# Transposing attention outputs to token rows: transpose instructions and a separate narrow logit product in place of one product with an identity-and-gate matrix

## The chip, the cores and the metric

The kernel runs on one core of one Trainium2 chip. The metric is the device time of one execution in microseconds, as the median of several runs. Below, PE is the matmul engine (its weight loads are listed apart as PEld), DVE, ACT and POOL are the vector, scalar and GpSimd engines, and SP issues most of the DMAs.

## What is computed

Linear attention over blocks feeds a top-1 mixture of experts. Shapes: q, k, v are (4, 8, 768, 64); x has N = 3072 tokens of 512 numbers; 8 experts, w1 (8, 512, 1024), w2 (8, 1024, 512).

```python
# attention, per batch and head, per block b of the sequence
intra = (qb @ kb.T * Dmask) @ vb
inter = (qb * lam_pow) @ kv_state
out[block] = intra + inter
kv_state = lam_block * kv_state + (kb * rev_pow).T @ vb
# x: the outputs of the 8 heads side by side, one row of 512 for each token
logits = x @ w_gate + modality_bias[modality_id]
e_idx = argmax(logits); gate_w = softmax(logits)[e_idx]
out[token] = gate_w * (relu(x @ w1[e]) @ w2[e])   # e = e_idx of the token
```

## The kernel before, in words

The kernel has two stages. **Attention** works on groups of 128 tokens (24 groups, numbered g), two groups to a pair (12 pairs, numbered j). Heads are taken in four pairs (`NP` = 4); the two heads of a pair lie in the two halves of the 128 partitions. Each pass of the loop `for j in range(1, pairs)` computes, on PE, the scores of two groups (`scores`, L239), what the carried state gives to the outputs (`from_state`, L285), what the masked scores give (`outputs`, L292, once for each group), and the products for the next state (`key_values`, L259). Between these stand four steps of the generator `turned(j - 1)`, which turn the outputs of the pair before from columns into token rows.

`outputs` leaves a group's result in SBUF as `xt`: 128 partitions (the two heads' 64 features), four head pairs, 128 tokens. Each step of `turned` calls `tokens`, which takes two of the four head pairs of one group: for each it makes two matmuls (L303), one for each half of 64 tokens, whose weights are that part of `xt` and whose moving operand is `iw`, 136 columns wide: a 128-wide identity (with its halves swapped for the second group of a pair, whose heads lie the other way round) and the 8 columns of the gate. So 4 head pairs x 136 = 544 numbers leave for each token: 512 features and four partial sums for the 8 logits. One copy for each step moves 2 x 136 columns from PSUM to SBUF (`xn`, L305), and after the second step of a group a DMA writes the rows, 544 numbers each, to the table `xs` in DRAM (L307). `gates` (L312) sums the four partial logits on DVE, and `route` picks the expert, two passes later.

PE's order is fixed by hand: `pinned` ties each instruction to the one before it on its engine. In a pass of the loop PE runs: scores, from_state, a step of `turned`, outputs of the first group, a step, outputs of the second group, a step, key_values, a step. PSUM tiles named "x" and "kv" have one buffer each; the steps use "x", and the second of them "kv" (as key_values does). "s" and "o" have two buffers. For the last pair the four steps stand after the loop, mixed with `turn_part` (L630), real transposes of the first gathered expert tile, and they use "s".

**Experts**: a tile of 256 tokens of one expert is gathered from `xs` by row (L595), turned by `turn_part`, and multiplied with `w1` and `w2`, each split in two parts (L643, L646, L647). Two tiles with few rows are done apart, with transposes (L689, L764) and on column tiles 64 and 32 wide (L678, L703).

Of the kernel before, what the change touches and what calls it, by code (L numbers as in the profile page):

```python
# [6 lines left out]
F32 = mybir.dt.float32  # L7
# [8 lines left out]
P = 128  # L16
B, H, S, D = 4, 8, 768, 64
NP = H // 2
NC = S // P
HB = 2  # L20
LOADS = 3
N = B * S
E, DM, F = 8, 512, 1024
# [10 lines left out]
LIST = THIN + MAX_WIDE + 2  # L34
PAD = 4096
SW = 8
ROW = DM + H // 2 * E
EMPTY = E * CAP // TT


def linear_attention_moe(tc, qkv, lam, modality, wg, mbias, w1, w2, out):
    nc = tc.nc
    with ExitStack() as ctx:
        const = ctx.enter_context(tc.tile_pool(name="const", bufs=1))
        dram = ctx.enter_context(tc.tile_pool(name="dram", bufs=1, space=bass.MemoryType.DRAM))
        ps = ctx.enter_context(tc.tile_pool(name="ps", bufs=1, space=bass.MemoryType.PSUM))
        work = ctx.enter_context(tc.tile_pool(name="work", bufs=2))
# [6 lines left out]
        def behind(later, first, wait=True):  # L54

            info = (mybir.DependencyInfo(mybir.DependencyClass.Sync, mybir.DependencyReason.DATA) if wait else
                    mybir.DependencyInfo(mybir.DependencyClass.NoSync, mybir.DependencyReason.SCHED_ONLY))
            tc.add_manual_dep(later.ins, first.ins.name, info, reason="order")


        halves2 = [slice(hl * D, (hl + 1) * D) for hl in range(2)]
        pins = {}

        def pinned(op):

            if op.ins.engine in pins:
                behind(op, pins[op.ins.engine], wait=False)
            pins[op.ins.engine] = op
            return op
# [48 lines left out]
        ident = const.tile([P, P], F32, name="ident")  # L118
        make_identity(nc, ident)

        wgt = const.tile([P, HB, NP, E], F32, name="wgt")
# [5 lines left out]
            return op  # L127


        iw = const.tile([P, HB, NP, P + E], F32, name="iw")  # L130
        onesb = const.tile([P, P], BF16, name="onesb")
        lowb = const.tile([P, P], BF16, name="lowb")
        desc = const.tile([P, E], F32, name="desc")
# [5 lines left out]
        modf = const.tile([P, 2, B * NC], F32, name="modf")  # L139
        xs = dram.tile([N, ROW], F32, name="xs")  # L140
        inv = dram.tile([E * CAP + TT, SW], I32, name="inv")
# [2 lines left out]
        pad = const.tile([P, some, SW], I32, name="pad")  # L144

        def identities():
            for blk in range(HB):
                nc.gpsimd.memset(iw[:, blk], 0.0)
                for hl, r in enumerate(halves2):
                    nc.gpsimd.tensor_copy(out=iw[r, blk, :, halves2[hl ^ blk]],  # L150
                                          in_=ident[r, r].unsqueeze(1).to_broadcast([D, NP, D]))

        def routing_constants():
            for to, src in ((mod, modality), (mb, mbias.partition_broadcast(P))):
# [53 lines left out]
        logits, ranked, fades = [], [], []  # L208
# [40 lines left out]
        def key_values(gs):  # L249

            kp = ps.tile([P, HB, NP, D], F32, name="kv", bufs=1)
            mm = None
            for g in gs:
                if g % NC == NC - 1 or g >= ng:
                    continue
                vt, kd = loaded(g)[2], kds[g // HB][:, g % HB]
                for p in range(NP):
                    for hl, r in enumerate(halves2):
                        mm = pinned(nc.tensor.matmul(kp[r, g % HB, p, :], kd[:, p, hl, :],  # L259
                                                     vt[:, (2 * p + hl) * D : (2 * p + hl + 1) * D], start=True, stop=True))  # L260
            return kp, mm
# [33 lines left out]
            pinned(nc.scalar.copy(out=xt, in_=op[blk]))  # L295
            return xt, mm

        def tokens(g, hf, xt, xn, xp):
            blk = g % HB
            for i in range(2):  # L300
                p = hf * 2 + i
                for r in halves2:
                    mm = pinned(nc.tensor.matmul(xp[r, i, : P + E], xt[:, p, r], iw[:, blk, p, :], start=True, stop=True))  # L303
            cp = nc.scalar.copy if g < ng - HB or (g == ng - 1 and hf == 0) else nc.vector.tensor_copy
            pinned(cp(out=xn[:, blk, 2 * hf : 2 * hf + 2, :], in_=xp[:, :, : P + E]))  # L305
            if hf == 1:
                nc.scalar.dma_start(out=xs[g * P : (g + 1) * P, :], in_=xn[:, blk].rearrange("t p d -> t (p d)"))  # L307
            return mm

        def gates(j, xn, lg):  # L310
            c = HB * j % NC
            logits.append(pinned(nc.vector.tensor_reduce(out=lg[:, c : c + HB, :], in_=xn[:, :, :, P:].rearrange("p b q e -> p b e q"),  # L312
                                                         axis=AX, op=ALU.add)))

        def route(b, lg):
# [273 lines left out]
        def groups(cols):  # L589

            return [(t, min(P, cols - t * P)) for t in range(-(-cols // P))]
# [11 lines left out]
        def fetch_regs(lst, i, always):  # L603
            er = value(lst, 0, i, E - 1)
            if always:
                return er, {}
            cr = value(lst, 2, i, 1)
            return er, {"cond": cr}
# [16 lines left out]
        def turn_part(i, cols, before=None, pin=False):  # L625
            tp = ps.tile([P, 2, TT], F32, name=("x", "kv")[i], bufs=1)
            for j in range(2):
                kc = 2 * i + j
                for t, m in groups(cols):
                    mm = nc.tensor.transpose(out=tp[:, j, t * P : t * P + m],  # L630
                                             in_=xg[t][:m, kc * (P + E) : kc * (P + E) + P], identity=ident[:m, :m])
                    if before is not None:
                        behind(mm, before, wait=False)
                    elif pin:
                        pinned(mm)
            return tp[:, :, :cols], xh[i][:, :, :cols], xl[i][:, :, :cols], pin
# [123 lines left out]
        def turn_few(x, rows):  # L760
            m = x.shape[-1]
            tp = ps.tile([P, KC, m], F32, name=("x", "kv")[m // XT], bufs=1)
            for kc in range(KC):
                pinned(nc.tensor.transpose(out=tp[:, kc, :], in_=rows[:, kc * (P + E) : kc * (P + E) + P],  # L764
                                           identity=ident[:m, :m]))
            return pinned(nc.vector.tensor_copy(out=x, in_=tp))

        def quarters(t):
            return [t[:, i] for i in range(4)]
# [5 lines left out]
        def parts(dt):  # L775

            return [work.tile([P, 4, KC, TT], dt, name=nm, bufs=1) for nm in ("w1h", "w1l")]

        w1h, w1l = (quarters(t) for t in parts(F32R))
        xg = [const.tile([m, ROW], F32, name=f"xg{t}") for t, m in groups(TT)]  # L780
        xq = [const.tile([m, ROW], F32, name=f"xq{i}") for i, m in enumerate((XT, FEW))]
        xh = [const.tile([P, 2, TT], F32R, name=f"xh{i}") for i in range(2)]
# [38 lines left out]

        ng = B * NC
        pairs, per = ng // HB, NC // HB
        kds, qds, xts, xns, lgs = {}, {}, {}, {}, {}
        early = SOON * per + 2
        routed, slots, placing = None, [], None

# [5 lines left out]


        def turned(j):
            xns[j] = work.tile([P, HB, NP, P + E], F32, name="xn", bufs=2)
            if j == pairs - 1:
                xp = [ps.tile([P, HB, 2, 256], F32, name="s", bufs=2) for _ in range(2)]
            for blk in range(HB):
                for hf in range(2):  # L840
                    if j < pairs - 1:
                        at = ps.tile([P, 2, 256], F32, name="kv" if hf and (j == pairs - 2 or j > 0 and blk == 0) else "x", bufs=1)
                    yield tokens(HB * j + blk, hf, xts[HB * j + blk], xns[j], xp[hf][:, blk] if j == pairs - 1 else at)

        def gated(j):
            b, c = divmod(j, per)
            if c == 0:
                lgs[b] = work.tile([P, NC, E], F32, name="lg", bufs=2)
            gates(j, xns.pop(j), lgs[b])
            return (b, *route(b, lgs.pop(b))) if c == per - 1 else None  # L850

        def more(j):
            if j < pairs:
                halves[j] = load_half(j)

        identities()
        clearing = clear_table(loads)
        c0, c1 = slice(0, 1), slice(1, 2)
# [17 lines left out]
        kp, _ = key_values([0])  # L876
# [1 line left out]
        xts[0], _ = outputs(0, pts[0], op)  # L878
        from_state(0, op, qds.pop(0))
        xts[1], _ = outputs(1, pts[1], op)  # L880
        pinned(nc.scalar.copy(out=iw[:, :, :, P:], in_=wgt))
        qds[1] = queries(1, c0, eng=nc.gpsimd)
        kp, _ = key_values([1])
        carried(1, kp)
        more(LOADS)
        for j in range(1, pairs):
# [20 lines left out]
            if j == 1:  # L907
                from_state(1, op, qds[1], range(1))
                next(turns)
                kp, _ = key_values(gs[:1])  # L910
                carried(gs[0], kp)
                keys(1, c1, kds[1])
            else:
                from_state(j, op, qds.pop(j))
                mm = next(turns)
# [7 lines left out]
            if j > 1:  # L923
                routed = gated(j - 2)
# [17 lines left out]
            kp, _ = key_values((gs[1], gs[1] + 1))  # L942
            mm = next(turns)
# [7 lines left out]
            if j == early:  # L951
                er, _ = fetch_regs(listA, 0, True)
# [4 lines left out]
            elif j == early + 2:  # L957
# [20 lines left out]
        hh, hl = ([t[:, i] for t in (work.tile([P, HB, 2, TT], F32R, name=f"{nm}{k}", tag=tag, bufs=2) for k in range(2))  # L978
                   for i in range(HB)] for nm, tag in (("hh", "pt"), ("hl", "kd")))
# [165 lines left out]
```

## Time and profile before

| | us |
|---|---|
| median of 3 runs | 412.56 (412.09 to 412.8) |
| the profiled execution | 410.96 |
| its span, first to last instruction | 408.6 |
| PE busy | 395.2 (97%) |
| DVE busy | 251.3 (61%) |
| ACT busy | 182.2 (45%) |
| POOL busy | 118.9 (29%) |

The profiled execution lasts 410.96 us, of which 2.4 us lie outside its span. Attention takes the span's first 105 us, the experts the rest; the last matmul ends near 397 us. Groups of instructions are named by line, engine and tiles; a matmul's form is given as rows x columns of the array that it uses (128*64 is all rows and half of the columns). A float32 matmul that is not a transpose is recorded as two instructions.

### The profile page before, as it was taken

How to read it: one execution, taken by the hardware profiler on the slowest of the kernel's cores; microseconds unless marked ns; L12 is line 12 of the kernel's file. 1: busy time of each engine (PE TensorE's matmuls, PEld its weight loads, DVE VectorE, ACT ScalarE, POOL GpSimd, SP SyncE). 2: the span in 40 equal slices, each digit the busy share in tenths (PEclk: the TensorE clock that was granted, in tenths of full speed). 3: DMA queues.
4: the chain of work that ended last, by engine and by line, in shares of the span. 5: the costliest groups of instructions: out<-in, count | busy, mean ns of one | idle time of the engine just before them, and what ended most of it. 6: DMA issues, size and time to landing. Idle time of an engine off the chain costs nothing.

```text
span 408.6 us, 9571 instructions
## 1 busy us (share of the span) xinstructions
PE 395.2 (97%) x3838; PEld 354.4 (87%) x3838; DVE 251.3 (61%) x430; ACT 182.2 (45%) x275; POOL 118.9 (29%) x125
## 2 busy tenths in 40 slices
PE   8999999999999999999999999999999999999990
PEld 3999899899998976989989898999989898998970
DVE  6777886978889714683746648273655738373610
ACT  2232243236654514582735547373644638273610
POOL 6701054452575610421230303122130402202000
PEclk9999999999999999999999999999999999999995
DMA  7999999994901291211073667111020211101000
GB/s 280 402 379 357 389 373 335 345 391 157 335 18 55 58 415 58 66 55 53 27 256 129 202 226 253 52 57 52 5 77 27 65 42 47 51 3 42 13 30 18
DMA packets 22374, 63.28 MB, mean 155 GB/s; under 512 B 6400, under 2 KB 6944, under 8 KB 20275
## 3 DMA queue, kind: packets, MB, share of 16 engines
q1 hardware_dynamic: 14000, 42.77, 28.9%
q0 software_dynamic: 4864, 13.15, 9.6%
q10 hardware_dynamic: 3458, 6.69, 4.3%
q8 instruction: 32, 0.52, 0.5%
q14 instruction: 20, 0.16, 0.1%
HBM read 90.87 MB, written 14.07 MB: 257 GB/s over the span
## 4 chain that ended last, share of the span: by engine, by line
PE 45%; issue 34%; POOL 7%; DMA 6%; DVE 4%; ACT 1%; POOLq 1%; SPq 1%; another core or an unknown queue 0%; DVEq 0%
PE s L239 5%; POOL out_dram L719 4%; PE o L292 4%; PE s L643 4%; PE s L646 4%; PE s L647 4%; PE x L303 3%; DMA idx<-inv 3%; PE o L285 3%; PE o L643 3%; PE o L646 3%; PE o L647 3%; POOL xg L595 2%; PE kv L259 2%; DMA xg<-xs,idx 2%
## 5 line engine op out<-in xcount | busy, mean ns | idle before, releaser
L643 PE MATMUL s<-xh,w1h 128*128 128x256 f32 x384 | 108.8, 283 | 0.0
L646 PE MATMUL s<-xl,w1h 128*128 128x256 f32 x384 | 108.5, 282 | 0.0
L647 PE MATMUL s<-xh,w1l 128*128 128x256 f32 x384 | 107.9, 281 | 0.0
L661 DVE SCALAR_TENSOR_TENSOR hl<-s,hh 128x512 fp32r<-128x512 f32 x48 | 33.2, 691 | 85.4 <-ACT hh L660 85.4
L643 PE MATMUL o<-w2h,hh 128*128 128x512 f32 x192 | 75.8, 395 | 0.0
L647 PE MATMUL o<-w2h,hl 128*128 128x512 f32 x192 | 74.8, 390 | 0.0
L646 PE MATMUL o<-w2l,hh 128*128 128x512 f32 x192 | 74.8, 389 | 0.0
L647 PEld LDWEIGHTS s<-xh,w1l 128*128 128x128 f32 x384 | 72.8, 190 | 0.0
L643 PEld LDWEIGHTS s<-xh,w1h 128*128 128x128 f32 x384 | 72.0, 187 | 0.9 <-ACT xn L305 0.3
L646 PEld LDWEIGHTS s<-xl,w1h 128*128 128x128 f32 x384 | 72.2, 188 | 0.4
L560 DVE TENSOR_TENSOR w2l<-raw,w2h 128x1024 fp32r<-128x1024 f32 x48 | 58.8, 1225 | 11.2 <-ACT w2h L559 11.2
L660 ACT ACTIVATE hh<-s 128x512 fp32r<-128x512 f32 x48 | 28.8, 599 | 72.9 <-PE s L647 71.7
L560 DVE TENSOR_TENSOR w1l<-raw,w1h 128x1024 fp32r<-128x1024 f32 x46 | 53.6, 1218 | 2.1 <-ACT w1h L559 2.0
L559 ACT CAST w2h<-raw 128x1024 fp32r<-128x1024 f32 x48 | 49.9, 1039 | 0.0
L595 POOL DMA_INDIRECT xg<-xs,idx x20 | 24.6, 1230 | 85.7 <-PE kv L630 81.5
L719 POOL DMA_INDIRECT out_dram<-y,idx x18 | 26.4, 1469 | 77.8 <-ACT y L735 77.8
L559 ACT CAST w1h<-raw 128x1024 fp32r<-128x1024 f32 x46 | 45.3, 1064 | 0.2 <-ACT w1h L559 0.2
L647 PEld LDWEIGHTS o<-w2h,hl 128*128 128x128 f32 x192 | 36.0, 188 | 7.6
L643 PEld LDWEIGHTS o<-w2h,hh 128*128 128x128 f32 x192 | 36.1, 188 | 7.1
L646 PEld LDWEIGHTS o<-w2l,hh 128*128 128x128 f32 x192 | 36.1, 188 | 7.1
L396 POOL DMA_INDIRECT inv<-pay,sloti x24 | 29.2, 1218 | 18.5 <-PE kv L303 5.5
L305 ACT COPY xn<-x 128x272 f32<-128x272 f32 x33 | 12.8, 388 | 44.9 <-PE x L303 44.9
(220 smaller groups left out, 474.0 us busy)
## 6 DMA issues: line engine op xcount, KB each, us to landing
raw<-in_w_dram SPq DMA_DIRECT2D x52, 1024.0 KB
load<-in_qkv_dram SPq DMA_DIRECT2D x8, 2048.0 KB
xs<-xn ACTq DMA_DIRECT2D x24, 272.0 KB
load<-in_qkv_dram SPq DMA_DIRECT2D x10, 512.0 KB
load<-in_qkv_dram SPq DMA_DIRECT2D x3, 1024.0 KB
w2f<-in_w_dram SPq DMA_DIRECT2D x2, 1024.0 KB
w1h<-in_w_dram SPq DMA_DIRECT2D x2, 1024.0 KB
inv<-pad SPq DMA_DIRECT2D x2, 196.0 KB
```

What stands on the lines that cost most here:

```text
L239: pinned(nc.tensor.matmul(sp[:, hl, p, :], kt[r, p, :], qt[r, p, :], start=True, stop=True))
L292: mm = pinned(nc.tensor.matmul(op[blk][halves2[hl ^ blk], p, :], vt[:, (2 * p + hl) * D : (2 * p + hl + 1) * D], pt[:, hl, p, :], start=(g ...
L396: sc = nc.gpsimd.indirect_dma_start(out=inv, out_offset=bass.IndirectOffsetOnAxis(ap=at, axis=0), in_=pay[:, c, :], in_offset=None)
L559: cp = nc.scalar.copy(out=hi, in_=src)
L560: df = nc.vector.tensor_tensor(out=lo, in0=src, in1=hi.bitcast(F32), op=ALU.subtract)
L595: last = nc.gpsimd.indirect_dma_start(out=(to or xg)[t][:m], out_offset=None, in_=xs[:rows, :], in_offset=bass.IndirectOffsetOnAxis(ap=idx ...
L643: mm = pinned(nc.tensor.matmul(out, ah, bh, start=first, stop=False))
L646: pinned(nc.tensor.matmul(out, ah, bl, start=False, stop=False))
L647: return pinned(nc.tensor.matmul(out, al, bh, start=False, stop=last))
L660: act = nc.scalar.activation(out=hh[i], in_=hp, func=AF.Relu)
L661: low = nc.vector.scalar_tensor_tensor(out=hl[i], in0=hp, scalar=0.0, in1=hh[i].bitcast(F32), op0=ALU.max, op1=ALU.subtract)
L719: sc = nc.gpsimd.indirect_dma_start(out=out, out_offset=bass.IndirectOffsetOnAxis(ap=idx[:, t, 0:1], axis=0), in_=y, in_offset=None, bound ...
```

## The change

`tokens` is split into three parts. `logit_parts` multiplies the outputs of both groups of a pair by the gate alone: `gw` holds the gate in 32 columns (8 of them used, the rest zero) for each head pair, and four matmuls, one for each head pair, write the four 32-wide column tiles of the array, so that the partial logits come out as columns. A copy brings them to SBUF (`lgt`), `logit_rows` turns them with two transposes and copies the 64 numbers of each token that count. `token_rows` turns one group's outputs with four 128x128 transposes into one bank of PSUM; one copy moves it out, or two for the second group, with the halves swapped. Rows in `xs` have 512 numbers in place of 544, and all readers of `xs` take 128-wide pieces. The four steps of `turned` become: logit_parts, token_rows of the first group, logit_rows, token_rows of the second group. The constant `iw` and its making on POOL go; `gw` is a memset and one copy.

```diff
-ROW = DM + H // 2 * E
+ROW = DM
+EW = 32
-        iw = const.tile([P, HB, NP, P + E], F32, name="iw")
+        gw = const.tile([P, HB, NP, EW], F32, name="gw")
         def identities():
-            for blk in range(HB):
-                nc.gpsimd.memset(iw[:, blk], 0.0)
-                for hl, r in enumerate(halves2):
-                    nc.gpsimd.tensor_copy(out=iw[r, blk, :, halves2[hl ^ blk]],
-                                          in_=ident[r, r].unsqueeze(1).to_broadcast([D, NP, D]))
+            nc.gpsimd.memset(gw, 0.0)
-        def tokens(g, hf, xt, xn, xp):
-            blk = g % HB
-            for i in range(2):
-                p = hf * 2 + i
-                for r in halves2:
-                    mm = pinned(nc.tensor.matmul(xp[r, i, : P + E], xt[:, p, r], iw[:, blk, p, :], start=True, stop=True))
-            cp = nc.scalar.copy if g < ng - HB or (g == ng - 1 and hf == 0) else nc.vector.tensor_copy
-            pinned(cp(out=xn[:, blk, 2 * hf : 2 * hf + 2, :], in_=xp[:, :, : P + E]))
-            if hf == 1:
-                nc.scalar.dma_start(out=xs[g * P : (g + 1) * P, :], in_=xn[:, blk].rearrange("t p d -> t (p d)"))
+        def logit_parts(j, at):
+            for blk in range(HB):
+                for p in range(NP):
+                    mm = pinned(nc.tensor.matmul(at[p * EW : (p + 1) * EW, blk * P : (blk + 1) * P], gw[:, blk, p, :],
+                                                 xts[HB * j + blk][:, p, :], start=True, stop=True, tile_position=(0, p * EW)))
+            lgt = work.tile([P, HB, P], F32, name="lgt", bufs=1)
+            pinned(nc.scalar.copy(out=lgt.rearrange("x b t -> x (b t)"), in_=at[:, : HB * P]))
+            return lgt, mm
+        def logit_rows(j, at, lgt):
+            for blk in range(HB):
+                mm = pinned(nc.tensor.transpose(out=at[:, blk * P : (blk + 1) * P], in_=lgt[:, blk, :], identity=ident))
+            xls[j] = work.tile([P, HB, NP, E], F32, name="xl8", bufs=2)
+            pinned(nc.scalar.copy(out=xls[j], in_=at[:, : HB * P].rearrange("t (b q e) -> t b q e", b=HB, q=NP)[:, :, :, :E]))
+            return mm
+        def token_rows(j, at, blk, xn, copy):
+            g = HB * j + blk
+            xt = xts[g]
+            for p in range(NP):
+                mm = pinned(nc.tensor.transpose(out=at[:, p * P : (p + 1) * P], in_=xt[:, p, :], identity=ident))
+            if blk == 0:
+                pinned(copy(out=xn[:, blk], in_=at))
+            else:
+                to, fr = (v.rearrange("t (a h d) -> t a h d", a=NP, h=2) for v in (xn[:, blk], at))
+                for hl in range(2):
+                    pinned(copy(out=to[:, :, hl], in_=fr[:, :, 1 - hl]))
+            nc.scalar.dma_start(out=xs[g * P : (g + 1) * P, :], in_=xn[:, blk])
             return mm
...
         def turned(j):
...
+            def bank(n):
+                if j == pairs - 1:
+                    return spare[n // 2][:, n % 2]
+                second = n % 2 and (j == pairs - 2 or j > 0 and n == 1)
+                return ps.tile([P, DM], F32, name="kv" if second else "x", bufs=1)
+
+            lgt, mm = logit_parts(j, bank(0))
+            yield mm
+            yield token_rows(j, bank(1), 0, xn, nc.vector.tensor_copy if j == pairs - 1 else nc.scalar.copy)
+            yield logit_rows(j, bank(2), lgt)
+            yield token_rows(j, bank(3), 1, xn, nc.scalar.copy)
```

## Rows read from the trace of the kernel before

**Rows 1.** The page: granted TensorE clock in 40 slices of the span, in tenths.
```profile
PEclk9999999999999999999999999999999999999995
```

**Rows 2.** One stretch: length; busy PE, PEld, DVE, ACT, POOL; clock; DMA share; GB/s.
```profile
31.37:39.06 7.69, 7.69 (x146) 7.21 (x146) 5.47 (x7) 2.52 (x6) 0.62 (x1) 1.00 0.98 345
```

**Rows 3.** Chain of waits, pass j = 3: start us, length us, what.
```profile
31.37 1.99 PE s L239 x32
33.35 1.02 PE o L285 x16
34.38 0.61 PE x L303 x8
34.99 0.87 PE o L292 x16
...
37.66 0.93 PE kv L259 x32
38.59 0.47 PE x L303 x8
```

**Rows 4.** Chain of waits, the last pair's steps after the loop.
```profile
102.08 0.79 PE x L630 x4
102.86 0.61 PE s L303 x8
103.48 0.59 PE kv L630 x4
```

**Rows 5.** Chain of waits in the expert stage: transposes; matmuls behind 32-wide ones.
```profile
157.90 0.58 PE s L689 x4
158.48 0.44 PE x L630 x4
...
165.06 0.32 PE s L643
165.38 0.12 PE s L646
```

**Rows 6.** PE in order of time, expert stage: start us, length us, instruction, form, count.
```profile
163.11 1.95 PE L703 MATMUL o<-w2f,hnt 128*32 128x128 f32 x64
164.99 0.39 PE L643 MATMUL s<-xh,w1h 128*128 128x256 f32 x1
```

**Rows 7.** Chain of waits near the start: key_values and outputs of one group.
```profile
10.54 0.61 PE kv L259 x16
...
13.05 1.02 PE o L292 x16
14.07 0.46 PE kv L259 x16
```

**Rows 8.** Waits from 7 to 105 us: who for whom, us in total, times, longest.
```profile
PEld kv L259 <- DVE oh L336: 0.4, 1, 0.4
PEld x L303 <- ACT xn L305: 0.4, 2, 0.2
PEld s L643 <- ACT xn L305: 0.3, 1, 0.3
PEld kv L259 <- issue: 0.3, 1, 0.3
...
PE o L285 <- DVE state L270: 0.2, 1, 0.2
...
PEld x L630 <- DMA xg<-xs,idxA: 0.2, 1, 0.2
```

**Rows 9.** Groups of instructions by line: busy us, mean ns; idle before, releasers.
```profile
L295 ACT COPY xt<-o 128x512 f32<-128x512 f32 x24 | 14.1, 586 | 13.6 <-PE o L292 13.6
L305 ACT COPY xn<-x 128x272 f32<-128x272 f32 x33 | 12.8, 388 | 44.9 <-PE x L303 44.9
...
L229 POOL TENSOR_TENSOR qd<-load,pq 128x512 f32<-128x512 f32 x3 | 3.9, 1288 | 6.7 <-PE o L285 4.3 <-ACT pq L93 2.3
...
L560 DVE TENSOR_TENSOR xl<-kv,xh 128x512 fp32r<-128x512 f32 x3 | 2.1, 693 | 0.6 <-ACT xh L559 0.6
```

More of the change, by code (lines that the diff above doesn't have):

```diff
@@ L311, in gates @@
             c = HB * j % NC
-            logits.append(pinned(nc.vector.tensor_reduce(out=lg[:, c : c + HB, :], in_=xn[:, :, :, P:].rearrange("p b q e -> p b e q"),
+            logits.append(pinned(nc.vector.tensor_reduce(out=lg[:, c : c + HB, :], in_=xn.rearrange("p b q e -> p b e q"),
                                                          axis=AX, op=ALU.add)))
@@ L630, in turn_part @@
                     mm = nc.tensor.transpose(out=tp[:, j, t * P : t * P + m],
-                                             in_=xg[t][:m, kc * (P + E) : kc * (P + E) + P], identity=ident[:m, :m])
+                                             in_=xg[t][:m, kc * P : (kc + 1) * P], identity=ident[:m, :m])
                     if before is not None:
@@ L763, in turn_few @@
             for kc in range(KC):
-                pinned(nc.tensor.transpose(out=tp[:, kc, :], in_=rows[:, kc * (P + E) : kc * (P + E) + P],
+                pinned(nc.tensor.transpose(out=tp[:, kc, :], in_=rows[:, kc * P : (kc + 1) * P],
                                            identity=ident[:m, :m]))
@@ L823, in linear_attention_moe @@
         pairs, per = ng // HB, NC // HB
-        kds, qds, xts, xns, lgs = {}, {}, {}, {}, {}
+        kds, qds, xts, xls, lgs = {}, {}, {}, {}, {}
         early = SOON * per + 2
@@ L835, in turned @@
         def turned(j):
-            xns[j] = work.tile([P, HB, NP, P + E], F32, name="xn", bufs=2)
+            xn = work.tile([P, HB, DM], F32, name="xn", bufs=2)
             if j == pairs - 1:
[L838 to L843, printed above, removed]
+                spare = [ps.tile([P, 2, DM], F32, name="s", bufs=2) for _ in range(2)]
+            def bank(n):
[8 more added lines that the diff above has]
+            yield token_rows(j, bank(3), 1, xn, nc.scalar.copy)
         def gated(j):
@@ L848, in gated @@
                 lgs[b] = work.tile([P, NC, E], F32, name="lg", bufs=2)
-            gates(j, xns.pop(j), lgs[b])
+            gates(j, xls.pop(j), lgs[b])
             return (b, *route(b, lgs.pop(b))) if c == per - 1 else None
@@ L880, in linear_attention_moe @@
         xts[1], _ = outputs(1, pts[1], op)
-        pinned(nc.scalar.copy(out=iw[:, :, :, P:], in_=wgt))
+        pinned(nc.scalar.copy(out=gw[:, :, :, :E], in_=wgt))
         qds[1] = queries(1, c0, eng=nc.gpsimd)
```

## The prediction

> **What bounds the kernel now.** I read the page first. PE is busy 97% of the span, as the small table says, and its clock is granted in full, the upper of its two levels, in every slice but the last [rows 1]. The table of stretches says the same for one pass of the attention loop: PE is busy 7.69 of 7.69 us, ACT 2.52 and DVE 5.47 [rows 2]. The 13.4 us in which PE is idle lie almost all at the span's two ends. So a microsecond added to or taken from PE's own order in attention should reach the end one for one, and what other engines do counts only where PE waits for them.
>
> Then I read the chain of waits for one undisturbed pass [rows 3]. The reader is to see that the pieces add up to the pass without a gap, and that two steps doing the same work do not cost the same: the step of `turned` behind from_state takes 0.61, the one behind key_values 0.47. The list of forms gives the difference. Outputs, key_values and the steps all use the array as 128*64; scores uses 64*128 and from_state 64*64. The step that costs 0.61 is the first in a new form. The same extra shows wherever the form changes: transposes (128*128) behind steps take 0.59, and behind other transposes 0.44 [rows 4, 5]; a step behind transposes 0.61 [rows 4]; key_values behind scores 0.61 and behind outputs 0.46; outputs behind from_state 1.02 against 0.87 elsewhere [rows 3, 7]. Every time it is 0.15 us, with all operands long there. That is the price of a **change of form**, and the change makes many of them.
>
> **The change part by part.**
>
> *Removed.* Four steps for each of 12 pairs, 0.464 each without the change of form (between the 0.46 and 0.47 of the rows) [rows 3, 4]: 1.86 us a pair.
>
> *Added matmuls.* Transposes: 0.44 for four [rows 5], so 0.44 + 0.44 + 0.22 for the ten of a pair, 1.10 us. The gate's product: 8 matmuls with 32-wide weights and 128 moving columns, 16 recorded instructions. The thin tile has exactly that form: 64 of them from 163.11 to 164.99 [rows 6], 1.88 us, less 0.15 for entering the form, 0.027 each: 0.43. Together 1.53. Work alone falls by **0.33 a pair, 4.0 in all**.
>
> Of this the row for transposes is the surest. The Trainium skill (Perfetto Trace Analysis, section Transposes) asks for real transposes in place of a standard matmul, because they skip arithmetic. The rows agree on the work, 0.11 a transpose. By that rule alone the kernel would end 4.0 us earlier; by the rows for changed forms it does not, as follows.
>
> *Changes of form.* Before, an ordinary pass goes 64*128, 64*64, then 128*64 to its end: three changes. After, it goes scores 64*128, from_state 64*64, logit_parts 128*32, outputs 128*64, transposes 128*128, outputs, transposes, key_values, transposes: nine. Eight passes gain 6 each. The first pass (from_state in two pieces) gains 5. The pass that also counts tiles between a step and outputs gains 4, as that matmul is 128*128 already; the last pass has no key_values and gains 4. Behind the loop the last pair loses 3: steps mixed with transposes before, [rows 4], now nearly all transposes. That is 48 + 5 + 4 + 4 - 3 = 58 changes at 0.15: **+8.7 us**. Bounds: nothing, if weights for the next form can be loaded under the last matmuls, and 0.20, by the first expert matmul behind the 32-wide ones, which takes 0.32 where the next takes 0.12 [rows 5]; I take 0.15, which all the other rows give.
>
> *Waits of before that slower PE work covers.* PE waited in attention 0.4 for ACT's copies, 0.4 for the DVE's routing, 0.3 more at key_values, 0.2 for the state, 0.2 for the first gathered rows, 0.3 before the first expert matmul [rows 8]: 1.8. The routing and the 0.3 at key_values come from DVE chains that start at scores; PE comes 0.5 later to the same place. The wait for copies goes, since key_values itself now costs 0.15 more while the copy of 64 numbers is shorter than that of 272. The first expert matmul waited for a copy out of "s" that is now made earlier. The state's I leave. That is -1.6, with 0 and -1.8 as ends.
>
> *New waits.* In "x", logit_rows is followed by key_values and then token_rows, which needs the bank back. Counted from the end of the second outputs in an ordinary pass: ACT copies `xt` until 0.65 (0.59) [rows 9], then the 64 numbers until about 0.95 (no more than the 0.39 for 272 numbers); PE comes at 0.37 + 1.08 = 1.45. In passes with one group's key_values it comes at 0.98, with nothing to spare. At key_values the "kv" bank is needed 1.4 us after token_rows of the first group; its copy (0.59) lies behind one `xt` copy (0.59) and is out in about 0.7. So none in the loop. Behind the loop one: `xh` and `xl` of the first expert tile come from ACT (0.59) and DVE (0.69) [rows 9], in line with a 0.69 copy of tokens on DVE, while PE now needs them some 0.7 sooner: +0.4.
>
> *At no cost.* ACT gets about 0.4 us more a pair, two copies of half a row among it, and has 5 of 7.7 us free [rows 2]. POOL loses the making of `iw`, four copies and two memsets; POOL waits for `pq` at that time, so nothing starts sooner [rows 9]. The DMAs on ACT's queue stay two a pair, of 256 KB in place of 272; at the 345 GB/s of that stretch [rows 2] the 24 save 1.2 us of DMA time, hidden under PE, whose only wait for rows is the 0.2 above. Gathers shrink alike. The scatters of slots on POOL, tied to the last matmul of a step, move by a few tenths and no PE instruction waits for them in attention.
>
> *Sum.* -4.0 + 8.7 - 1.6 + 0.4 = **+3.5 us**: the profiled execution goes from 410.96 to 414.5. The median of the runs is 1.6 above that execution, so 412.56 becomes **416.1**.
>
> **The rivals.**
>
> *The changes of form are hidden* (the other side). If PE loaded the first weights of the next form under the last matmuls of the former, only the work would count: -4.0, and with it 0.3 before the first expert matmul, 408.3. It decides from 4.0/58, that is below 0.07 a change. For it: 128*128 to 128*128 between lines costs nothing [rows 5]. Against: every change timed above costs 0.15 or more, with nothing to wait for.
>
> *Hidden in part.* With DVE's chains as the true pace of several passes, or changes at 0.10, the sum is -4.0 + 5.8 - 1.6 + 0.4 = +0.6: 413.2, no change that can be told. For it: DVE is busy 5.47 of 7.69 us [rows 2] and paces at least two passes. Against: the undisturbed passes have no wait at all to give.
>
> *Copies become the bound.* If a bank comes back late in each pass, by the 0.4 that one plain copy takes [rows 9], the ten passes add 4: 420.1. For it: "x" now serves three uses in a row with the copies of `xt` between. Against: 0.5 to spare in ordinary passes, worked out above.
>
> *The clock.* The granted clock stayed at its upper level where four groups of transposes, fourteen in all, follow one another [rows 1, 5]. If it fell to the lower level under the transposes of each pass, these would take twice as long: 12 x 1.10 = 13 us, near 429. The Trainium skill (TensorE: Matmul & The Clock Gate, Part 4) says that transposes do not count as activity for the clock as matmuls do. The trace does not bear it out so far: 0.11 a transpose at full clock; but a tenth of attention was never transposes before.
>
> **How the numbers follow.** Forecast 0.64; hidden 0.10; hidden in part 0.08; copies 0.13; clock 0.05. The likeliest case alone spans 414 (changes at 0.13, all waits regained: -4.0 + 7.5 - 1.8 = +1.7) to 419 (changes at 0.18, half of the waits regained: -4.0 + 10.4 - 0.8 + 0.4 = +6.0). To leave out no more than 2 in 10 the range takes in most of the copies' case and the edge of hidden in part: 413.2 to 420.5. A measurement tells 0.2%, 0.8 us, from no change: faster 0.10, same 0.08, slower 0.82.
>
> **What would show it.** In the chain of waits after: an ordinary pass of about 8.28 us for 7.70, with logit_parts 0.59, outputs 1.02 twice, token_rows 0.59, logit_rows 0.37, key_values 1.08, token_rows 0.59. Steps at 0.44, 0.22 and outputs at 0.87 would show the hidden case. PE waiting for ACT's copies before token_rows would show the copies' case, and a granted clock under 1.00 between 7 and 110 us the clock's. The first expert matmul should start about 109 us, for 105.2 before, and the expert stage take the same time. I am wrong if entering 128*32 or leaving transposes between attention matmuls costs otherwise than in the few rows seen, or if the DVE chains hold PE up more than reckoned.

## The result and the profile after

The changed kernel takes **416.39 us** (median of 4 runs, 415.29 to 416.68); the kernel before took 412.32 beside it (4 runs, 411.21 to 412.8). The ratio is 1.0098, with a 95% interval of 1.0069 to 1.0126: slower by 2.8 to 5.2 us. The forecast was 416.1, within 413.2 to 420.5. The profiled execution took 415.29 us, with a span of 413.5 and PE busy 398.9 us of it; the forecast for it was 414.5.

The page's line of granted clocks, as in [rows 1]:

```profile
PEclk9999999999999999999999999999999999999997
```

Transposes in every pass of attention have not lowered the clock. The chain of waits for pass j = 3, as in [rows 3] (start us, length us, what):

```profile
30.92 1.99 PE s L236 x32
32.90 1.02 PE o L282 x16
33.92 0.57 PE x L298 x16
34.50 1.02 PE o L289 x16
35.52 0.59 PE kv L315 x4
36.11 1.02 PE o L289 x16
37.13 0.37 PE x L306 x2
37.50 1.08 PE kv L256 x32
38.59 0.59 PE x L315 x4
```

Here L236 is scores, L282 from_state, L298 logit_parts, L289 outputs, L315 token_rows, L306 logit_rows and L256 key_values. The reader is to see two things. There is no wait in the chain, as before; and outputs, untouched by the change, costs 1.02 where [rows 3] has 0.87, key_values 1.08 where they have 0.93. The pass takes 8.25 us for 7.69. The table of stretches for that pass (columns as in [rows 2]) says that PE is still the only full engine, with ACT at 2.88 of 8.25 us:

```profile
30.92:39.17 8.25, 8.25 (x140) 6.85 (x140) 5.21 (x6) 2.88 (x7) 0.62 (x1) 1.00 0.98 338
```

Where the time went, by the ends of PE's matmuls in the two profiled executions (us):

| stretch | before | after | difference |
|---|---|---|---|
| start to the end of the scores of pass j = 1 | 16.52 | 15.36 | -1.16 |
| ten passes, j = 1 to 10, from scores' end to scores' end | 80.05 | 83.95 | +3.90 |
| last pass and the last pair's steps, to the end of the first expert matmul | 8.98 | 10.16 | +1.17 |
| experts, to the end of the last matmul | 291.93 | 293.54 | +1.61 |
| behind the last matmul, with what lies outside the span | 13.48 | 12.29 | -1.19 |
| sum | 410.96 | 415.29 | +4.33 |

The passes carry what the prediction is about. The other four rows add up to 0.43 only because they cancel. The +3.90 belongs to this pair of profiles: in the second profiles of the two kernels, further down, the ten passes take 81.37 and 84.39, +3.02, because waits differ between executions, those of the kernel before above all. The chain at the end of attention shows two pieces of the other rows, where [rows 4] has three groups in a row without a gap (here L645 is the transposes of the gathered tile, L658 the first expert matmul):

```profile
99.57 1.31 PE o L282 x30
100.88 0.32 issue
101.20 0.29 PE o L282
...
106.08 0.60 PE x L645 x4
106.71 0.59 ACT xh L574
...
107.33 0.70 DVE xn L317
...
108.42 0.22 ACT xl L308
...
108.68 0.66 PE s L315 x4
109.34 0.12 PE s L658
```

First, from_state of the last pass is broken by an idle piece for which the profile shows nothing that PE waited for ("issue"); all of it takes 1.93 us, for 1.03 before. Second, the last token_rows waits for a copy of ACT. The waits from 7 to 110 us name it, where [rows 8] has other waits (who for whom, us in total, times, longest):

```profile
PEld s L315 <- ACT xl L308: 1.0, 1, 1.0
...
PE s L315 <- ACT xl L308: 0.8, 1, 0.8
```

The expert stage, which should not change, has two pieces of its own. The waits from 110 to 180 us show the first, a wait for DVE behind the ranking matmuls; at that place the end of a matmul is 0.55 us later than the 3.9 us that were brought along:

```profile
PE s L658 <- DVE hl L676: 0.8, 1, 0.8
```

And the waits from 165 to 180 us show ACT held up by something outside of the core's own engines ("remote"), after which PE is 1.0 us later than before:

```profile
ACT yn L722 <- remote: 3.4, 1, 3.4
...
ACT hh L675 <- remote: 1.1, 1, 1.1
```

### The profile page after: what moved, and what is told of

The parts are those of the page before. It is cut to its first block, busy times and chain, and to the rows that moved or that the text cites. A ratio compares the mean times of both kernels' runs of the same rounds, so it can differ in the third digit from the quotient of the medians.

```text
span 413.5 us, 9441 instructions
## 1 busy us (share of the span) xinstructions
PE 398.9 (96%) x3766; PEld 349.8 (85%) x3766; DVE 250.7 (61%) x428; ACT 186.6 (45%) x289; POOL 116.6 (28%) x120
## 2 busy tenths in 40 slices
DMA packets 22373, 62.49 MB, mean 151 GB/s; under 512 B 6399, under 2 KB 6943, under 8 KB 20274
## 4 chain that ended last, share of the span: by engine, by line
PE 45%; issue 34%; POOL 6%; DMA 6%; DVE 3%; another core or an unknown queue 1%; ACT 1%; SPq 1%; POOLq 1%; ACTq 0%; DVEq 0%
PE o L289 5%; PE s L236 5%; POOL out_dram L734 4%; PE s L658 3%; PE s L662 3%; PE s L661 3%; DMA idx<-inv 3%; PE o L282 3%; PE o L658 3%; PE o L662 3%; PE o L661 3%; PE kv L256 3%; POOL xg L610 2%; DMA xg<-xs,idx 2%
## 5 line engine op out<-in xcount | busy, mean ns | idle before, releaser
L658 PE MATMUL s<-xh,w1h 128*128 128x256 f32 x384 | 108.9, 284 | 1.2 <-DVE hl L676 0.8
L661 PE MATMUL s<-xl,w1h 128*128 128x256 f32 x384 | 108.5, 282 | 0.0
L658 PE MATMUL o<-w2h,hh 128*128 128x512 f32 x192 | 75.8, 395 | 0.0
L661 PE MATMUL o<-w2l,hh 128*128 128x512 f32 x192 | 74.8, 390 | 0.0
L658 PEld LDWEIGHTS s<-xh,w1h 128*128 128x128 f32 x384 | 72.0, 187 | 2.1 <-DVE hl L676 1.0
L661 PEld LDWEIGHTS s<-xl,w1h 128*128 128x128 f32 x384 | 72.2, 188 | 0.4
L575 DVE TENSOR_TENSOR w2l<-raw,w2h 128x1024 fp32r<-128x1024 f32 x48 | 58.8, 1224 | 10.7 <-ACT w2h L574 10.4
L575 DVE TENSOR_TENSOR w1l<-raw,w1h 128x1024 fp32r<-128x1024 f32 x46 | 53.6, 1219 | 6.5 <-ACT yn L722 3.3
L658 PEld LDWEIGHTS o<-w2h,hh 128*128 128x128 f32 x192 | 36.1, 188 | 7.1
L661 PEld LDWEIGHTS o<-w2l,hh 128*128 128x128 f32 x192 | 36.1, 188 | 7.1
L750 ACT ACTIVATE y<-o,idx 128x512 f32<-128x512 f32 x18 | 12.4, 689 | 43.5 <-PE o L662 42.7
```

What stands on the lines that cost most here:

```text
L575: df = nc.vector.tensor_tensor(out=lo, in0=src, in1=hi.bitcast(F32), op=ALU.subtract)
L658: mm = pinned(nc.tensor.matmul(out, ah, bh, start=first, stop=False))
L661: pinned(nc.tensor.matmul(out, ah, bl, start=False, stop=False))
```

## The experiments

**My theory:** a pass costs its work plus 0.15 us for each change of array form; the change takes 0.33 us of work from a pass and adds six changes. **Rivals:** the added time is waits for copies (a bank that comes back late), or it is the transposes themselves, or the row width does something.

### The price of a change of form, in the kernel before

Nothing of the computation is changed; a transpose of the identity that nobody reads goes in front of each of the 48 steps.

```diff
             blk = g % HB
+            pinned(nc.tensor.transpose(out=xp[:, 0, :P], in_=ident, identity=ident))
             for i in range(2):
```

> The kernel before, with one 128x128 transpose of the identity put in front of each of the 48 steps, into PSUM that the step then overwrites: nothing of the computation changes. Work added: 48 x 0.109 = 5.2 us. Changes of form added: seven in an ordinary pass, about 81 in all, 12.2 us at 0.15. Theory: 17.4 less about 1.5 of waits that go under, +16, 428. Rival, changes of form are hidden under the last matmuls: only the transposes' own 5.2 or less, at most 417.5.

430.86 us against 412.51 (ratio 1.0433, 1.0401 to 1.0465): +18.4 us for 48 transposes, 2.4 more than the +16 expected. In the profiled execution (431.95 for 410.96) the ten passes take 15.55 us more, the last pass with the steps behind it 2.93, and the expert stage, where no transpose was added, 3.12. The chain of one pass (L300 is the added transpose, L304 the step, L292 outputs):

```profile
33.81 1.99 PE s L239 x32
35.80 1.02 PE o L285 x16
36.82 0.26 PE x L300
37.08 0.61 PE x L304 x8
37.69 0.87 PE o L292 x16
...
41.19 0.93 PE kv L259 x32
42.12 0.26 PE x L300
42.38 0.61 PE x L304 x8
```

The single transpose takes 0.26, which is 0.11 and 0.15; the step behind key_values takes 0.61 where [rows 3] has 0.47, also 0.15 more. Outputs stays at 0.87, as it follows a step of its own form. The pass has ten changes for three and 0.44 us more of work: 7.69 + 7 x 0.15 + 0.44 = 9.18, and it takes 9.18. With changes hidden it would have been 8.13. The step behind the added transpose writes the same PSUM bank as that transpose, with no copy between them; so the extra needs neither a new bank nor a late copy.

### The same instructions in fewer forms

If the form decides, the changed kernel's own instructions in another order must give the time back. In the four kernels that follow the transposes of a pair stand together behind key_values, in one form. A pass has then five changes: scores, from_state, logit_parts, both outputs with key_values, all transposes. The bare sum is 8.25 - 4 x 0.15 = 7.65 us, below the 7.69 before.

**First try:** both groups' rows go to the two halves of one "s" tile (`xt` has a fourth buffer, since it is read later).

```diff
-            xt = work.tile([P, NP, P], F32, name="xt", bufs=3)
+            xt = work.tile([P, NP, P], F32, name="xt", bufs=4)
...
+            if j < pairs - 1:
+                both = ps.tile([P, 2, DM], F32, name="s", bufs=2)
+                for blk in range(HB):
+                    token_rows(j, both[:, blk], blk, xn, nc.scalar.copy)
+                yield logit_rows(j, bank(2), lgt)
+                return
...
             write_slot(mm)
-            next(turns)
```

> The same instructions as the changed kernel, but in each pass the eight transposes of tokens and the two of logits stand together behind key_values (and one more buffer for xt, so that no copy waits for them). Changes of form fall from nine to five in an ordinary pass, 39 fewer in all. Theory, each change costs 0.15 us on PE: 5.9 us less than the changed kernel, 410.5, and up to 1.6 back where DVE's chains hold PE up again, so 410.5 to 412; an ordinary pass 7.65 us for 8.25. Rival, changes of form are hidden and the 4 us come from copies and banks that are late: no gain, 416 or more, since ten transposes in a row press more on ACT and on the banks.

421.32 us, ratio 1.0211 (1.0188 to 1.0234): slower than the change itself, and far from the 410.5 to 412 expected. An ordinary pass takes 8.55. The waits of weight loads and of matmuls from 7 to 115 us:

```profile
PEld s L315 <- ACT xn L317: 10.0, 11, 0.9
...
PE s L315 <- ACT xn L317: 7.4, 11, 0.7
```

In each of the eleven passes the second group's transposes wait for the copy of the first group's, although they write the other half of the tile, which nobody reads. The four forms are saved, and 0.89 a pass is paid for that: 7.66 + 0.89 = 8.55.

**Second try:** all eight transposes of a pair ahead of both copies.

```diff
+                for blk in range(HB):
+                    mm = token_turn(j, both[:, blk], blk)
+                for blk in range(HB):
+                    token_copy(j, both[:, blk], blk, xn, nc.scalar.copy)
```

> The regrouped kernel with all eight transposes of a pass written ahead of the two copies, so that the second four do not wait for the copy out of the other half of their PSUM tile. Theory: the regrouped kernel lost 0.68 us or more on PE in each pass to that wait and gained what the four changes of form cost; without it an ordinary pass takes 1.985 + 1.034 + 0.574 + 1.897 + 0.93 + 1.02 + 0.22 = 7.66 us (8.25 in the changed kernel, 7.69 before), and the whole 412, with 0.8 and 1.4 still lost in the two passes where key_values comes too early for DVE. Rival: changes of form are not what the pass pays for, and the pass stays above 8.

418.93 us, ratio 1.0149 (1.0111 to 1.0188). The wait between the two groups is gone, and the ordinary pass falls to 8.06, but not to 7.66: the tile is now kept until both copies are out, and the second half of the next scores needs it. The weight loads' waits from 7 to 115 us:

```profile
PEld s L236 <- ACT xn L330: 5.0, 9, 1.1
```

Two passes with routing work were far longer (9.43 for j = 5, 9.97 for j = 8).

**Third try:** in those two passes key_values moves behind the transposes, and behind the loop the last logit_rows and token_rows go ahead of the copies.

```diff
-            next(turns)
-            kp, _ = key_values((gs[1], gs[1] + 1))
-            mm = next(turns)
+            ranked_here = j in (per + 2, 2 * per + 2)
+            if ranked_here:
+                mm = next(turns)
+            kp, km = key_values((gs[1], gs[1] + 1))
+            if not ranked_here:
+                mm = next(turns)
```

> The same, with key_values behind the transposes in the two passes that rank tokens (so that DVE's chain is done when PE comes), and with logit_rows and the last token_rows of the last pair ahead of their copies. Theory: 1.9 less in the two passes, 0.5 to 0.8 less behind the loop: 410 to 411, under the kernel before by some 0.4%. Rival: DVE's chains take the place of the removed waits behind the loop, and the gain there is nothing: 411 to 412.

415.94 us, ratio 1.0084 (1.0057 to 1.0111): no gain over the change, where 410 to 411 was expected. j = 5 came down to 7.61 and j = 8 to 9.29, but j = 6 went up from 8.63 to 9.39: there the chain of waits stops at the copies out of "s", after a piece of 0.46 with no releaser. The 0.40 for "s" in each ordinary pass was still there, which I had left out of the expectation.

**Fourth try:** as the third, with the transposes in the two "o" buffers, which are separate tiles and free at that time.

```diff
-                both = ps.tile([P, 2, DM], F32, name="s", bufs=2)
+                both = [ps.tile([P, DM], F32, name="o", bufs=2) for _ in range(HB)]
                 for blk in range(HB):
-                    mm = token_turn(j, both[:, blk], blk)
+                    mm = token_turn(j, both[blk], blk)
```

> As the last regrouped kernel, but the eight transposes of a pass write the two buffers of o (free since xt was copied) and not one of the two buffers of s. Theory: what is left of the expected gain there is a wait of the second scores for the copies out of s, 0.40 in every pass; without it an ordinary pass is the bare sum of PE's groups, 7.66 us, and the whole 4 us less, 411.5 to 412.5, level with the kernel before. Rival: the wait moves to from_state, which needs o, and the pass stays near 8.

413.02 us (12 runs) against 412.1 (23 runs), ratio 1.0008 (0.9987 to 1.003): level with the kernel before, 0.5 above the expected range. Its chain of an ordinary pass:

```profile
31.20 1.99 PE s L236 x32
33.19 1.02 PE o L282 x16
34.21 0.57 PE x L298 x16
34.78 1.90 PE o L289 x32
36.68 0.93 PE kv L256 x32
37.61 1.03 PE o L315 x8
38.64 0.22 PE x L306 x2
```

7.66 us, with no wait. Both outputs together take 1.90 for 2 x 1.02, key_values is back at 0.93, and the eight transposes take 1.03 for 2 x 0.59. The ordinary passes are 0.03 shorter than before, no more. The ten passes take 80.70 us, between the 80.05 and 81.37 of the two profiles of the kernel before. It too has passes with waits: 9.21 for j = 8, where the matmul that counts tiles waits for a chain on DVE that began at scores, 0.3 to 0.65 more in three others, and from_state of the last pass again (2.08).

### The last pair's steps

logit_rows of the last pair moves ahead of the transposes of the second gathered half.

```diff
         split(*rows0)
+        next(turns)
         rows1 = turn_part(1, TT, pin=True)
         split(*rows1)
         next(turns)
-        next(turns)
```

> The changed kernel with one swap behind the loop: logit_rows of the last pair ahead of the second turn_part, so that its copy on ACT stands ahead of the second cast of xh. Theory: the last token_rows waits for that copy, because both write halves of one PSUM tile, and the late copies of tokens on ACT then delay the casts of w1 that cost 0.55 behind the rank matmuls: 0.8 to 1.3 less, 415.1 to 415.6. Rival: DVE's chain of xl and w1l sets the pace there anyway, and the swap gives under 0.3.

415.74 us, ratio 1.0075 (1.0052 to 1.0098), against 1.0091 for the changed kernel on the same chip: 0.4 us by the medians, less than the intervals can tell apart. In the trace the wait did go: the last token_rows takes 0.52 us, wait included, for 1.45. Of these 0.93 us, 0.41 comes back at the next expert matmul, now for `xl` of the gathered tile, as the chain shows (L575 makes it, L661 uses it):

```profile
107.28 0.60 PE x L645 x4
...
107.91 0.59 ACT xh L574
...
108.53 0.69 DVE xn L317
109.22 0.61 DVE xl L575
...
109.87 0.39 PE s L661
```

The wait behind the ranking matmuls falls from 0.55 to 0.20, as the token copies leave ACT earlier. From the scores of the last pass to the last matmul the swap saves 0.8 to 1.0 us (302.68, for 303.70 and 303.50 in the two profiles of the changed kernel), as the expectation has it; in these profiles the whole does not show it, because the kernel starts 1.2 us later, which the section on both kernels once more explains. So two waits lay behind each other: the one for the copy of logit_rows, and behind it the chain of casts and copies that the prediction's +0.4 is about.

### The width of the rows

The changed kernel with rows of 544 numbers, the last 32 zero. First with a memset on POOL in each pass:

```diff
-ROW = DM
+ROW = DM + H // 2 * E
...
+            nc.gpsimd.memset(xn[:, :, DM:], 0.0)
```

> The changed kernel with rows of 544 numbers in the table again, the last 32 of each zero and read by nobody. Theory: no difference to the changed kernel, 416.0 to 416.8, since PE waits for rows nowhere but at the first tile. Rival: the shorter rows gave back 0.5 us or more through DMA traffic, and this is slower by that.

424.48 us, ratio 1.0298 (1.0246 to 1.035), but the width is not what is measured. The waits over the whole span:

```profile
POOL xn L852 <- DMA xs<-xn: 30.8, 5, 8.2
...
PE o L282 <- DVE state L271: 3.9, 2, 2.1
```

The kernel is 8 us slower than the change, against the expectation: the memset waits for the DMA that still reads the buffer, POOL's part of the carried state queues behind it, and from_state waits for that. So again, with two fixed buffers zeroed once at the start:

```diff
+        xns = [const.tile([P, HB, ROW], F32, name=f"xn{i}") for i in range(2)]
...
+            for x in xns:
+                nc.gpsimd.memset(x[:, :, DM:], 0.0)
...
-            xn = work.tile([P, HB, DM], F32, name="xn", bufs=2)
+            xn = xns[j % 2]
```

> The changed kernel with rows of 544 again, the 32 idle numbers now zeroed once at the start in two fixed buffers, so that POOL has nothing to do for them in the loop (in the first try a memset on POOL in each pass waited for the DMA of the rows and held up the state). Theory: no difference to the changed kernel, 416.0 to 416.8. Rival: shorter rows gave back 0.5 us or more, and this is slower by that.

416.13 us (10 runs), ratio 1.0091 (1.0066 to 1.0116), the same as the changed kernel. The page counts 63.27 MB moved for 62.49, and no wait of PE for a DMA shows.

### Both kernels once more

What differs between two profiles may belong to the executions. So each kernel was profiled again.

> The changed kernel unchanged, for a second profile. Theory: ordinary passes of the loop take 8.25 us again, and about 416.4 in all. In the first profile four deviations from the forecast stand beside these passes: the start 1.2 us shorter, 0.9 lost in from_state of the last pass, 1.1 lost before the last token_rows, 1.6 lost in the expert stage (0.55 behind the rank matmuls, 1.07 near 176 us). Those that belong to the program come back here at the same place; those that belong to one execution (I expect the start, the 0.9 and the 1.07) do not. Rival: all of them belong to the change and all come back.

416.12 us, ratio 1.0091 (1.006 to 1.0123). The ten passes agree with the first profile within 0.01, except for 0.2 in each of the last two. The long from_state, the wait of the last token_rows, the wait behind the ranking matmuls, ACT's wait and the shorter start were all there again; the expectation had the start, from_state and ACT's wait down as belonging to one execution.

> The kernel before unchanged, for a second profile. Its first profile was one of its fastest executions (410.96 for a median of 412.5) and had none of the 1.0 us that ACT loses near 170 us in every profile taken since, waiting for nothing that the profile names. Theory: that wait belongs to the executions of either kernel, and shows here too, with the first matmul of the experts at the same distance from the scores of the first pass as in the first profile (89.0 us). Rival: it came with the change; then this profile has none.

413.78 us in one run. It has ACT's wait of 3.4 us, the first row below (waits from 165 to 180 us), which the first profile of before had not, and PE is 1.05 us later there. So that 1.0 us comes without the change too. The first matmul of the experts ends 90.8 us behind the scores of the first pass, not 89.0 as expected: pass j = 9 lost 1.4 us that it had not lost in the first profile, and pass j = 4 had none of the 0.5 that it lost there. The expert stage takes 293.41 us, as in the second profile of the changed kernel (293.43): it has ACT's wait, and 0.43 lost at the 32-wide matmuls of a thin tile in place of the 0.55 behind the ranking matmuls. Its start is like that of the first profile: the eight matmuls that the kernel runs on a constant before there is data take 3.56 us (3.59 in the first), as the second row says (PE in order of time: start, length, instruction):

```profile
ACT yn L707 <- remote: 3.4, 1, 3.4
```

```profile
3.75 3.56 PE L819 MATMUL o<-busy 128*128 128x512 bf16 x8
```

In the changed kernel the same eight take 2.44 and 2.39 in its two profiles. Here is the first, and then all twelve matmuls of this kind in both kernels (first profiles; ns, shortest, middle and longest, then the us in which they start):

```profile
3.75 2.44 PE L834 MATMUL o<-busy 128*128 128x512 bf16 x8
```

```profile
L834 PE MATMUL o<-busy x12: 379/570/634, 1.4 to 5.8; 128*128 128x512 bf16 x12
L819 PE MATMUL o<-busy x12: 606/634/634, 1.4 to 6.7; 128*128 128x512 bf16 x12
```

In the kernel before they start 0.43 us apart to the end. In the changed kernel the last four, from 4.94 us on, follow at 0.21, so the engine goes from the lower to the upper of its clock's two levels (1.2 and 2.4 GHz) in between. The trace says when: its record of the granted clock begins, at full, at 4.9 us in the changed kernel and at 7.3 in the kernel before. Ahead of the first record the table of stretches prints 1.00, which is no reading there. What PE does up to that moment is the same in both: matmuls on a constant and two small ones. The record begins at 4.8 and 4.9 us in the two profiles of the changed kernel and at 6.4 to 8.0 in the ten others, among them seven variants of the change, and the scores of pass j = 1 end later by half of the delay: 15.31 us at 4.8, 16.09 at 6.4, 16.52 at 7.3, 16.85 at 8.0. So the 1.2 us are a clock that rose earlier, ahead of any instruction of PE that the change touches. What sets the moment no run shows.

## Why the prediction was right

**What bounds the kernel** held. PE is busy 8.25 of 8.25 us in the pass, and the ordinary pass grew by what was added to its order.

**The work of a pass** was right: -0.33. Without its changes of form the pass before is 7.69 - 3 x 0.15 = 7.24, the fourth reordered kernel 7.66 - 5 x 0.15 = 6.91. The rule of the Trainium skill (Perfetto Trace Analysis, section Transposes) holds for this part: the logit products and ten transposes of a pair are cheaper than its four steps with the identity.

**The changes of form** were right in number and price. The first and third row of the table set the two works, at the price of 0.15; the second and fourth then test that price:

| kernel | work | changes | sum | measured pass |
|---|---|---|---|---|
| before | 7.24 | 3 | 7.69 | 7.69 |
| changed | 6.91 | 9 | 8.26 | 8.25 |
| changed, in fewer forms ("o") | 6.91 | 5 | 7.66 | 7.66 |
| before, with lone transposes | 7.24 + 0.44 | 10 | 9.18 | 9.18 |

The same instructions, 8.25 in one order and 7.66 in another, show that it is the order and not the transposes: outputs, token_rows, key_values and logit_rows each lose 0.15 once. Transposes are not needed for it either: outputs costs 1.02 behind logit_parts as behind transposes. Every group of the pass came out within 0.02 of the forecast. The hidden rival (408.3) and the one hidden in part fall with the first row of the single transpose. Why a change costs 0.15, no run shows.

**The covered waits** went the way that was forecast, but their size can't be tested. For the ten passes the forecast's terms give -0.33 x 10 + 57 x 0.15 and at most -1.1 of waits: +4.15 or a little more; measured +3.90. The passes that had waits grew by less than the others: +0.29, +0.09 and +0.12 for j = 2, 4 and 8, against +0.56 for j = 3. But the waits change from execution to execution. The 0.5 of j = 4 is missing in the second profile of the kernel before, and 1.4 in j = 9 is only there; between the second profiles the ten passes grow by 3.02.

**The copies** did not become the bound in this order: in the loop PE's matmuls never wait for ACT, and its weight loads once in each of the two profiles, for 0.2 us. The rival was well founded though. Where the transposes stood together in one tile, it came true at 421.3, near the 420.1 that it gave.

**The clock** (429) did not fall: 1.00 in the pass. What this rival made of the page of the Trainium skill (TensorE: Matmul & The Clock Gate, Part 4) did not come: ten transposes, 1.1 us of work, among the other matmuls of each pass left the clock where it was. The page's statement on transposes is not tested by that, as no run has a long stretch of transposes alone.

**The end of attention** was mis-sized. The terms that lie there (work of two pairs, 4 - 3 changes, 0.5 of waits regained, +0.4) give -0.6; measured +1.17. The wait behind the loop is 1.0 and not 0.4: I had seen the chain of casts, but not that token_rows waits for the copy of logit_rows out of the other half of its tile, and that this copy is queued behind a cast on ACT. With it the waits of before were not regained there. The other 0.9 is the broken from_state of the last pass. It takes 1.8 to 2.0 us in every profile of the changed order, 1.73 and 2.08 in the third and fourth of the reordered kernels, and 1.72 in the kernel before with the added transposes, which has none of the new steps; it takes 1.17 in the first two reordered kernels and 1.03 in both profiles of the kernel before. In those two no DMA moves anything during it, in all the others 146 to 251 GB/s; but the first two reordered kernels have that traffic too. The profile names nothing that PE waited for. **Its cause stays open.** The first expert matmul started at 109.10 us, as forecast (109), only because the start was shorter by about as much as the end of attention was longer.

**"The expert stage takes the same time"** failed by 1.61 us in the first pair of profiles: 0.55 behind the ranking matmuls, a wait that repeats and shrinks to 0.20 when the token copies come sooner, and 1.07 behind ACT's wait, which is found in the kernel before as well. Between the second profiles the stage takes the same time, 293.41 and 293.43, as the kernel before loses 0.43 there at another place. **The ends** had no term in the forecast: start and finish are 2.35 shorter in this pair of profiles. Of that, 1.16 is the clock that rose earlier. What lies outside the span is 1.76 us on average in the four runs of the changed kernel and 2.11 in 48 of the kernel before, and 1.7 to 1.8 in every variant of the change; the cause stays open.

So the sum was right to 0.8 us in the profiled execution, and that is in part luck. The end of attention and the expert stage cost 3.4 us more than forecast, the ends gave back 2.35 that the forecast had no reason for, and the passes 0.25. What was right for its reason is the ordinary pass: 8.25 for a forecast of 8.28, with both profiles of each kernel in agreement on it.

## What to carry to other kernels

Before a product is split into cheaper kinds, count in PE's order how often the array's form changes, and price each change by a row of the trace where the same step costs more behind another form; here 0.15 us each outweighed 0.33 us of saved work in every pass. When kinds must mix, put all of one form side by side, but look at the PSUM tiles that this needs: of the 0.59 that a pass gained, a wait for the copy out of the other half of a shared tile first took 0.89, and a wait of scores for that same tile then took 0.40, until the transposes went to two tiles that nothing else needed soon. And take a second profile of both kernels before a difference of a microsecond is explained, outside the changed stage above all.

## What the runs showed of the hardware

- A change of form costs 0.15 us wherever the same group also stands behind its own form: 128*64 behind 64*64, 64*128, 128*32 and 128*128 (outputs 1.02 for 0.87, key_values 0.61 for 0.46 and 1.08 for 0.93), and 128*128 behind 128*64 and 128*32 (0.59 and 0.60 for 0.44); for one transpose (0.26 for 0.11) as for 32 matmuls. Into 128*32 it is 0.14 by an estimate from the thin tile of [rows 6] (0.57 for 0.43). Scores and from_state never stand behind their own form, so their price is not shown.
- A transpose of a float32 128x128 piece takes 0.11 us among its like, with the granted clock at 1.00 throughout.
- The same eight matmuls at the start took 2.39 and 2.44 us in the two profiles of the changed kernel and 3.17 to 3.59 in the ten others, as the record of the full clock begins at 4.8 and 4.9 us or at 6.4 to 8.0.
- ACT waited 3.3 to 3.4 us at one place of the expert stage for something that the profile puts outside the core's engines, in one of two profiles of the kernel before and in both of the changed one; PE was 1.0 later behind it.
- A memset on POOL in each pass that waits for a DMA cost the kernel 8 us (424.48 for 416.13 to 416.39), through the state that queues behind it.
